# Reordering three pieces of a fused scan and expert kernel: a ScalarE copy in the start, a state update and a gated layer on VectorE

## The chip, the cores and the metric

The kernel runs on one core of a Trainium2 chip. The metric is the device time of one execution in microseconds, as the median of several runs; lower is better. Everything is computed in fp32.

## The reference, cut to what matters

Two stages run one after the other. The first is a gated linear recurrence over time (a "mamba2" scan), computed in chunks. The second is a sum over four expert networks, each weighted by a probability.

```python
# scan: batch 4, 8 heads, 768 steps, head_dim 32, d_state 16
for c in range(nc):                       # per chunk of the sequence
    cum = np.cumsum(log(a)[chunk])
    M = (C @ B.T) * exp(cum_i - cum_j) * causal
    y = M @ x + (C @ state) * exp(cum)
    state = exp(sum) * state + sum_j(B_j x_j * exp(cum_last - cum_j))
...
# experts: 3072 tokens, D = 256, 4 experts, F = 1024
p = probs / (probs.sum(-1) + 1e-9)
for e in range(4):
    h = np.maximum(x @ w1[e], 0.0)
    out += p[:, e:e+1] * (h @ w2[e])
```

The `x` of the second stage is the output `y` of the first, with its heads laid side by side.

## The kernel before, in words

**Tiling.** The 3072 tokens are 24 chunks of 128. Four chunks, one of each sequence, make a block `k` of 512 tokens, so there are six blocks (`NBLK`). A block goes through eight steps (`SPB`): four experts, each in two halves of its hidden layer. A step has the number `n`, 0 to 47, and `r = n % 8` is its place in the block. While the experts of block `k` run, the chunks of block `k + 1` go through the scan in between, so the scan has to be woven into the experts' steps.

**The experts' step.** Each step computes two matrix products by a seven-product (Strassen-like) scheme. The first layer is `fmul(n, 1..7)` (L500, matmuls on L514), which accumulates in two PSUM banks named X and Y. The second layer of the step before is `smul(n - 1, 1..7)` (L584, matmuls on L599), which accumulates in four banks `acc0` to `acc3`. Each of these fourteen products is two 128x256 matmuls with 128x128 weights, and the profile records each matmul as two passes. Between the two layers VectorE and ScalarE do this:

- `snap` (L518): ScalarE copies the bank X as it stands to SBUF.
- `total` (L523, operation on L526): VectorE adds the bank Y and a snap and writes `z`. `total(n, 7, "22")` must have read Y before `fmul(n, 3)` may write on in it.
- `gated` (L528, L536): VectorE takes max(., 0) of its source and multiplies by the gate. `gated(n, "21", "X")` reads the bank X itself; the others, `"12"` among them, read a `z` in SBUF.
- `diff` (L540, L543): VectorE subtracts two gated layers, which gives T1 to T4 for the second layer. T2 and T4 are put in a list `late` and run in the next step, after its first gated layer.

**The scan's parts in the steps.** In steps with r = 0, 2, 4 and 5 a chunk's decays are computed (`decay_part` 0 and 1, scans on L355). In steps with r = 3 and r = 6, called scored here, two chunks are scored: `masks` on ScalarE (L369), `decay_part(c, 2)` on VectorE (two scans `dec`, L338, and on GpSimd `cts`, L341), `scores` on TensorE (L384) and `masked` on VectorE (eight multiplies, L396). `scores` works in four groups of 32 rows, one for each pair of heads, and its four results go into four banks: two of the pool `ps_att`, then Y, then X. So the third group has to wait until `total(n, 6, "12")` has read Y, and the fourth until `gated(n, "21", "X")` has read X. In the steps after (r = 4 and 7) `outputs` (L441, L453) makes the scan's result from them.

**The carried state.** `carry(c)` (L471) makes a chunk's state for the next block: a 32x32 block transpose (L477), from block 1 on a multiply-add with the old state (L479), and a multiply by a mask (L484), all on VectorE. It is put at the end of `late`, one chunk in a step, as long as there are chunks in `states`. In a scored step there is one in n = 3 and n = 6 (chunks 2 and 4), and then in each r = 6 up to n = 30: in n = 3, 6, 14, 22 and 30. The chunks of the last block have no state to hand on, and their `carry` does nothing.

**The start.** Before the steps the first chunks are scanned with little to overlap. `masks(0)`, `scores([0])` and `decays(0)` run first. One of the four score results of a chunk is not multiplied by VectorE: `aside(c, q)` (L398) copies it to SBUF on ScalarE (L403), and GpSimd multiplies it (L404). ScalarE also issues two stores, `acut_d` and `ac_d` (L279), which hold the decays that later chunks load.

**What sets the order.** The program is scheduled by hand (`manual_schedule`): each engine executes its instructions in the order in which these lines issue them, and waits on semaphores where a tile is not yet written or not yet free. SyncE issues the loads, in that same order.

Of the kernel before, what the change touches and what calls it, by code (L numbers as in the profile page):

```python
# [17 lines left out]
def kernel(  # L18
# [295 lines left out]
    def spread(c, homes):  # L314


        s = st[c]
        s["a"] = []
        for q, (pool, tag) in enumerate(homes):
            k = slice(32 * q, 32 * q + 32)  # L320
            b = pool.tile([P, NT * P], FP32, tag=tag, name="a")
            nc.tensor.matmul(  # L322
                out=b, lhsT=ones[k], rhs=a_q[k, c].rearrange("p t s -> p (t s)"),
                start=True, stop=True, tile_position=(32 * q, 0))
            s["a"].append(b)

    def decays(c):
        for part in range(3):
            decay_part(c, part)

    def decay_part(c, part):

        s = st[c]
        if part == 2:
            if c >= CPB:

                s["dec"] = dec = att.tile([HN, P], FP32, tag="dec", name="dec")
                nc.vector.tensor_tensor_scan(  # L338
                    out=dec, data0=s["ah"], data1=zeros, initial=1.0, op0=ALU.mult, op1=ALU.add)
                s["cts"] = cts = att.tile([HN, NT, P], FP32, tag="cts", name="cts")  # L340
                nc.gpsimd.tensor_mul(cts, s["ctm"], dec.unsqueeze(1).to_broadcast([HN, NT, P]))  # L341
            return
        half = NH * P // 2
        if part == 0:
            if c >= SPREAD:
                s["a"] = [s["ab"][:, :half], s["ab"][:, half:]]
            LT = att.tile([P, NH * P], FP32, tag="LT", name="LT")
            s["LT"] = LT.rearrange("p (h s) -> p h s", h=NH)

            s["MT"] = att.tile([P, NH, P + N], FP32, tag="MT", name="MT")  # L350

        LT, w = s["LT"].rearrange("p h s -> p (h s)"), s["a"][0].shape[1]
        n = half // w
        for i in range(n * part, n * part + n):
            nc.vector.tensor_tensor_scan(  # L355
                out=LT[:, i * w:i * w + w], data0=s["a"][i],
                data1=ident.rearrange("p h s -> p (h s)")[:, :w], initial=0.0,
                op0=ALU.mult, op1=ALU.add)
        if part == 1 and c < NCH - CPB:
            nc.gpsimd.tensor_mul(  # L360
                s["MT"][:, :, P:], s["xb"][:, OB:OB + HN].rearrange("p (h n) -> p h n", h=NH),
                s["LT"][:, :, P - 1:P].to_broadcast([P, NH, N]))

    def masks(c):

        s = st[c]
        m = s["ctm"] = att.tile([HN, NT, P], FP32, tag="ctm", name="ctm")
        for t in range(NT):
            nc.scalar.mul(m[:, t], s["xb"][:, OCT:OCT + P], tmask[:, t:t + 1])  # L369

    def scores(cs, homes):

        for c in cs:
            st[c]["g"] = {}
        for r, (pool, tag) in enumerate(homes):
            g = pool.tile([P, len(cs), NT, P], FP32, tag=tag, name="g")
            for j, c in enumerate(cs):
                st[c]["g"][r ^ 2 * turned_round(c)] = g[:, j]
        for j, c in enumerate(cs):
            s = st[c]  # L380
            for r in range(NQ):
                k = slice(32 * r, 32 * r + 32)
                g = s["g"][r ^ 2 * turned_round(c)]
                nc.tensor.matmul(  # L384
                    out=g.rearrange("p t s -> p (t s)"), lhsT=s["xb"][k, OBT:OBT + P],
                    rhs=s["ctm"][k].rearrange("p t s -> p (t s)"),
                    start=(j == 0), stop=True, tile_position=(32 * r, 0),
                    skip_group_check=True)
# [9 lines left out]
    def aside(c, q):  # L398

        s = st[c]  # L400
        h = slice(NT * q, NT * q + NT)
        g = att.tile([P, NT, P], FP32, tag="gs", name="gs")
        nc.scalar.copy(out=g, in_=s["g"][q])  # L403
        nc.gpsimd.tensor_mul(s["MT"][:, h, 0:P], g, s["LT"][:, h])  # L404
# [123 lines left out]
    def gated(n, b, src):  # L528

        if n not in hid:  # L530
            hid[n] = {}
        h = hid[n][b] = ffn.tile([P, JJ, HB], FP32, tag="h" + b, name="h" + b)
        k, e = n // SPB, n % SPB // JJ
        half = int(b[1]) - 1
        g = gate[k, e].rearrange("p c s -> p (c s)")[:, half * HB:half * HB + HB]
        nc.vector.scalar_tensor_tensor(  # L536
            out=h, in0=first[n][src], scalar=0.0, in1=g.unsqueeze(1).to_broadcast([P, JJ, HB]),
            op0=ALU.max, op1=ALU.mult)
# [161 lines left out]
    def leave(k, c):  # L700

        for q in range(P // 32):
            for d in range(2):
                leave_part(k, c, q, d, nc.sync)

    def opened(n):

        fmul(n, 1)
        snap(n, 1)
        fmul(n, 2)  # L710
# [16 lines left out]
    masks(0)  # L727
    scores([0], homes)
    decays(0)
    masks(1)  # L730
    spread(1, banks)
    aside(0, 3)
    masked([0], (2, 0, 1))
    store_decays(0)
    turn_gates(ps_att, "att")
# [65 lines left out]
    late = []  # L801
    states = [2, 3]
    for n in range(PLAIN, NS):
        k, r = divmod(n, SPB)

        ahead = CPB * (k + 1)
        scanned = [ahead + d for d in {0: [0], 2: [1], 4: [2], 5: [3]}.get(r, [])]
        scored = [ahead + d for d in {3: [0, 1], 6: [2, 3]}.get(r, [])]
        done = [ahead + d for d in {4: [0, 1], 7: [2, 3]}.get(r, [])]
        if k == NBLK - 1:  # L810
            scanned, scored, done = [], [], []
        ending = r == 0 and k > 0
        e = r // JJ
        if r % JJ == 0 and n + JJ < NS:
            load_gate(*divmod(n // JJ + 1, E))
        if PLAIN + 2 < n + 2 < NS:
            load_w1(n + 2)
            load_w2(n + 2)
        opened(n)
        total(n, 1, "11")  # L820
        gated(n, "11", "z11")
        for work in late:
            work()
        if r == 1 and k > 0:
            combine(k - 1, 0)
            combine(k - 1, 1)
        for c in scanned:
            decay_part(c, 0)
        for c in scored:
            masks(c)  # L830
        if k > 0 and 2 <= r < CPB + 2:
            leave(k - 1, r - 2)
        smul(n - 1, 1)
        fmul(n, 6)
        snap(n, 6)
        smul(n - 1, 3)
        if ending:
            keep(k - 1, 0)
        if done:
            outputs(done)  # L840
            states.extend(done)
        fmul(n, 5)
        fmul(n, 7)
        snap(n, 7)
        total(n, 7, "22")
        smul(n - 1, 7)
        smul(n - 1, 5)
        if ending:
            keep(k - 1, 1)
        gated(n, "22", "z22")  # L850
        if r == 1 and k > 0:
            combine(k - 1, 2)
        for c in scanned:
            decay_part(c, 1)
        for c in scored:
            decay_part(c, 2)
        if n == PLAIN:
            sum_w2(0, 1)
        elif n == SPB - 4:
            sum_w1(n + 2)  # L860
        elif n >= SPB - 3:
            sum_w2(n)
        if n < CPB:
            load_chunk(n + CPB)
        for c in scanned if n >= CPB else []:
            if c + 2 < NCH:
                load_decays(c + 2)
        for c in done:
            if c + CPB < NCH:
                load_tokens(c + CPB)  # L870
                load_heads(c + CPB)
        fmul(n, 3)
        total(n, 6, "12")
        fmul(n, 4)
        gated(n, "21", "X")
        if not scored:
            gated(n, "12", "z12")
        if r == SPB - 1 and k < NBLK - 1:
            sums(k + 1)
        smul(n - 1, 6)  # L880
        if scored:
            scores(scored, ((ps_att, "att"), (ps_att, "att"), (ps_f, "Y"), (ps_f, "X")))
            masked(scored, (3, 2, 0, 1))
            gated(n, "12", "z12")
        smul(n - 1, 2)
        diff(n, "T3", "22", "12")
        smul(n - 1, 4)
        if n == PLAIN:
            sum_w2(1, 1)
        if n != SPB - 4:  # L890
            sum_w1(n + 2)
        if PLAIN < n < SPB - 4:
            sum_w2(n + 1)
        diff(n, "T1", "12", "11")
        if r == 1 and k > 0:
            turned_out(k - 1)
        late = [lambda n=n: diff(n, "T2", "22", "T1"), lambda n=n: diff(n, "T4", "21", "T2")]
        if states:
            late.append(lambda c=states.pop(0): carry(c))
# [48 lines left out]
```

## Time and profile before

| what | value |
|---|---|
| time, median of 5 runs | 638.64 us (638.58 to 641.01) |
| time of the profiled execution | 639.22 us |
| span of the profiled execution | 637.4 us, so 1.8 us lie around it |
| TensorE busy | 632.5 us, 99% of the span |
| TensorE weight loads busy | 537.2 us, 84% |
| VectorE busy | 483.4 us, 76% |
| ScalarE, GpSimd busy | 119.4 us and 112.0 us, 19% and 18% |
| granted TensorE clock | 1.000 |
| DMA | 190 GB/s over the span |

Times in the profile are microseconds from the start of the span. In the timeline a line gives the start, the time it took, the engine, the line of the kernel, the operation, its output and inputs, their shapes and the number of instructions that were merged. In brackets stands the idle time of the engine before it and what ended that idle time. The recorded end of a matmul is modelled and overlaps the next one, so the distance from start to start tells more of TensorE than the busy time does.

### The profile page before, as it was taken

What the parts mean: (1) busy time and instruction counts of PE and PEld (TensorE: products, weight loads), DVE (VectorE), ACT (ScalarE), POOL (GpSimd) and SP (SyncE); (2) the same over time, 40 slices, a digit from 0 to 9 for tenths busy, and PEclk for the clock granted to TensorE, in tenths of its full rate; (3) what the DMA queues carried; (4) which work ended last, traced back from release to release, by engine and by line L of the source; (5) the groups of instructions that cost most, each with busy time, mean ns of one, the idle gap of its engine ahead of it and who ended that gap; (6) DMA issues with size and microseconds to landing.
All of it is one profiled execution on the core that took longest, in us unless ns stands there. A gap on an engine that the chain in (4) does not pass through costs nothing.

```text
span 637.4 us, 9254 instructions
## 1 busy us (share of the span) xinstructions
PE 632.5 (99%) x3405; PEld 537.2 (84%) x3405; DVE 483.4 (76%) x812; ACT 119.4 (19%) x263; POOL 112.0 (18%) x163
## 2 busy tenths in 40 slices
PE   9999999999999999999999999999999999999997
PEld 5788887888888888888888888888888888888886
DVE  7869988888777788678687778778867677756555
ACT  4011221212111221122221221122111211111110
POOL 5788557020001002100002000000100000100001
PEclk9999999999999999999999999999999999999999
DMA  6998893855666292657284567639365644156001
GB/s 223 277 329 301 280 340 141 294 185 165 182 211 236 79 378 68 236 176 245 100 281 157 170 193 197 233 109 353 88 218 186 221 156 133 62 169 224 1 1 33
DMA packets 98224, 121.61 MB, mean 191 GB/s; under 512 B 29496, under 2 KB 81412, under 8 KB 98180
## 3 DMA queue, kind: packets, MB, share of 16 engines
q1 hardware_dynamic: 95224, 111.20, 53.2%
q0 software_dynamic: 2432, 9.50, 3.9%
q8 instruction: 27, 0.44, 0.3%
q10 hardware_dynamic: 524, 0.32, 0.2%
q14 instruction: 17, 0.14, 0.1%
HBM read 108.16 MB, written 12.83 MB: 190 GB/s over the span
## 4 chain that ended last, share of the span: by engine, by line
PE 98%; DVE 1%; ACT 0%; issue 0%; DVEq 0%
PE acc L599 43%; PE X L514 25%; PE Y L514 19%; PE g L384 2%; PE acc L580 2%; PE y L453 2%; PE X L563 1%; PE Y L563 1%; PE y L441 1%; PE t L720 1%; DVE hT L543 0%; PE a L322 0%; DVE h L536 0%; DVE z L526 0%; PE gp L300 0%
## 5 line engine op out<-in xcount | busy, mean ns | idle before, releaser
L526 DVE TENSOR_TENSOR z<-Y,snap 128x512 f32<-128x512 f32 x138 | 94.6, 685 | 117.2 <-ACT snap L521 66.3
L599 PE MATMUL acc<-hT,wt 128*128 128x256 f32 x736 | 181.0, 379 | 0.0
L521 ACT COPY snap<-X 128x512 f32<-128x512 f32 x138 | 80.8, 586 | 464.6 <-PE X L514 388.1
L599 PEld LDWEIGHTS acc<-hT,wt 128*128 128x128 f32 x736 | 139.8, 190 | 19.0
L599 PE MATMUL acc<-h,wt 128*128 128x256 f32 x552 | 142.5, 381 | 0.0
L514 PE MATMUL X<-yS,wt 128*128 128x256 f32 x552 | 141.7, 379 | 0.0
L599 PEld LDWEIGHTS acc<-h,wt 128*128 128x128 f32 x552 | 104.0, 190 | 17.0 <-issue 2.3
L514 PEld LDWEIGHTS X<-yS,wt 128*128 128x128 f32 x552 | 104.8, 190 | 14.5 <-issue 0.3
L536 DVE SCALAR_TENSOR_TENSOR h<-z,gate 128x512 f32<-128x512 f32 x138 | 99.0, 717 | 3.5 <-PE acc L580 0.4
L514 PE MATMUL Y<-yT,wt 128*128 128x256 f32 x368 | 94.6, 380 | 0.1
L514 PEld LDWEIGHTS Y<-yT,wt 128*128 128x128 f32 x368 | 68.7, 190 | 11.3 <-DVE z L526 0.8
L543 DVE TENSOR_TENSOR hT<-h,hT 128x512 f32<-128x512 f32 x92 | 65.2, 709 | 1.8
L543 DVE TENSOR_TENSOR hT<-h,h 128x512 f32<-128x512 f32 x92 | 65.1, 748 | 1.4
L355 DVE TENSOR_TENSOR_SCAN LT<-ab,ident 128x512 f32<-128x512 f32 x42 | 52.1, 1242 | 0.0
L514 PE MATMUL Y<-yS,wt 128*128 128x256 f32 x184 | 48.3, 385 | 0.0
L514 PE MATMUL X<-yT,wt 128*128 128x256 f32 x184 | 47.2, 379 | 0.0
L360 POOL TENSOR_TENSOR MT<-xb,LT 128x128 f32<-128x128 f32 x20 | 8.5, 427 | 207.4 <-DVE LT L355 102.5
L396 DVE TENSOR_TENSOR MT<-g,LT 128x256 f32<-128x256 f32 x94 | 32.4, 415 | 13.1 <-PE g L384 13.1
L514 PEld LDWEIGHTS Y<-yS,wt 128*128 128x128 f32 x184 | 34.1, 190 | 6.4 <-issue 2.2
L514 PEld LDWEIGHTS X<-yT,wt 128*128 128x128 f32 x184 | 35.0, 190 | 4.8
L536 DVE SCALAR_TENSOR_TENSOR h<-X,gate 128x512 f32<-128x512 f32 x50 | 34.3, 685 | 5.7 <-PE X L514 3.4
L341 POOL TENSOR_TENSOR cts<-ctm,dec 128x256 f32<-128x256 f32 x20 | 14.1, 724 | 129.1 <-DVE dec L338 129.1
(104 smaller groups left out, 324.5 us busy)
## 6 DMA issues: line engine op xcount, KB each, us to landing
wt<-in_w_dram SPq DMA_DIRECT2D x112, 256.0 KB
wt<-w_d SPq DMA_DIRECT2D x40, 640.0 KB
wt<-w_d SPq DMA_DIRECT2D x40, 512.0 KB
ab<-acut_d SPq DMA_DIRECT2D x21, 512.0 KB
gate<-p_d SPq DMA_DIRECT2D x23, 256.0 KB
w_d<-wt POOLq DMA_DIRECT2D x8, 640.0 KB, 4.1
wt<-in_w_dram SPq DMA_DIRECT2D x40, 128.0 KB
xb<-in_xbc_dram SPq DMA_DIRECT2D x14, 320.0 KB
```

The costliest lines, as they stand in the source:

```text
L341: nc.gpsimd.tensor_mul(cts, s["ctm"], dec.unsqueeze(1).to_broadcast([HN, NT, P]))
L355: nc.vector.tensor_tensor_scan(out=LT[:, i * w:i * w + w], data0=s["a"][i], data1=ident.rearrange("p h s -> p (h s)")[:, :w], initial=0.0, ...
L384: nc.tensor.matmul(out=g.rearrange("p t s -> p (t s)"), lhsT=s["xb"][k, OBT:OBT + P], rhs=s["ctm"][k].rearrange("p t s -> p (t s)"), start ...
L396: nc.vector.tensor_mul(s["MT"][:, h, 0:P], s["g"][q], s["LT"][:, h])
L453: nc.tensor.matmul(out=y[32 * q:32 * q + 32, t, 0:w], lhsT=s["xb"][:, h * D:h * D + D], rhs=s["MT"][:, NT * q + t, 0:w], start=(k == 0 and ...
L514: nc.tensor.matmul(out=f[bank][:, j], lhsT=wt1[n][:, w, j * P:j * P + P], rhs=rhs, start=(i in (1, 2, 5) and j == 0), stop=(j == JJ - 1), ...
L521: nc.scalar.copy(out=s, in_=first[n]["X"])
L526: nc.vector.tensor_add(z, first[n]["Y"], first[n][i])
L536: nc.vector.scalar_tensor_tensor(out=h, in0=first[n][src], scalar=0.0, in1=g.unsqueeze(1).to_broadcast([P, JJ, HB]), op0=ALU.max, op1=ALU. ...
L543: nc.vector.tensor_sub(h[o], h[x], h[y])
L563: nc.tensor.matmul(out=f[bank][:, j], lhsT=wt1[n][:, w, j * P:j * P + P], rhs=yT[k][:, i, cols], start=(i == 0 and j == 0), stop=(i == 1), ...
L599: nc.tensor.matmul(out=acc[k, u][:, half], lhsT=w2_op(n, w)[:, j], rhs=rhs[:, j], start=(begins and j == 0), stop=(n % SPB == SPB - 1 and ...
```

## The change

Three pieces of work change their place in the program's order. No instruction is added or removed. TensorE, GpSimd and SyncE keep their order; ScalarE's order changes in the start, and VectorE's in the scored steps.

1. In the start, `aside(0, 3)` moves in front of `masks(1)`. On ScalarE the copy of the fourth score result of chunk 0 then comes before the two masks of chunk 1.
2. In scored steps `carry` no longer runs with T2 and T4, in front of `total(n, 7, "22")`. It runs after that total and the gated layer `"22"`, in front of `decay_part(c, 2)`.
3. In scored steps `gated(n, "12", "z12")` runs before `masked` instead of after it, as it already does in all other steps.

```diff
     decays(0)
+    aside(0, 3)
     masks(1)
     spread(1, banks)
-    aside(0, 3)
     masked([0], (2, 0, 1))
...
         gated(n, "11", "z11")
-        for work in late:
+        for work in late[:2] if scored else late:
             work()
...
         for c in scanned:
             decay_part(c, 1)
+        for work in late[2:] if scored else []:
+            work()
         for c in scored:
             decay_part(c, 2)
...
         gated(n, "21", "X")
-        if not scored:
-            gated(n, "12", "z12")
+        gated(n, "12", "z12")
         if r == SPB - 1 and k < NBLK - 1:
             sums(k + 1)
         smul(n - 1, 6)
         if scored:
             scores(scored, ((ps_att, "att"), (ps_att, "att"), (ps_f, "Y"), (ps_f, "X")))
             masked(scored, (3, 2, 0, 1))
-            gated(n, "12", "z12")
         smul(n - 1, 2)
```

## The prediction

> **What bounds the kernel now.** I read the page first, then TensorE's busy time by stretch, then TensorE's and VectorE's timelines around the changed steps. The page and the stretches:
>
> ```profile
> PE 632.5 (99%) x3405; PEld 537.2 (84%) x3405; DVE 483.4 (76%) x812; ACT 119.4 (19%) x263; POOL 112.0 (18%) x163
> PE 98%; DVE 1%; ACT 0%; issue 0%; DVEq 0%
> ```
>
> ```profile
> 0.00:25.00 25.00, 23.69 (x173) 1.00 0.75 241
> 25.00:110.00 85.00, 84.86 (x472) 1.00 0.81 279
> 110.00:632.40 522.40, 522.40 (x2763) 1.00 0.53 175
> ```
>
> The columns of the second are the stretch, its length, TensorE's busy time, its clock and the DMA share. TensorE is the bound: from 110 us to 632.4 us it has no idle time. There is nothing to gain there, only something to lose. What idleness there is lies in the start (1.31 us) and in block 0's steps (0.14 us recorded).
>
> Of block 0, the chain of waits shows where VectorE gets onto the path, in step 6:
>
> ```profile
> 95.75 1.10 DVE hT L543
> ...
> 97.00 0.49 DVE S L479
> ...
> 97.52 0.29 DVE M L484
> 97.81 0.61 DVE z L526
> ...
> 98.47 1.13 PE Y L514 x4
> ```
>
> T4 (hT), then the carried state (S, M), then `total(6, 7)` (z), and only then does TensorE get the bank Y for `fmul(6, 3)`. TensorE's timeline gives the price. In step 14 the eight passes in front start at 199.90 and Y at 201.63: 1.73 us, or 0.216 a pass. In step 6 they start at 96.44 and Y at 98.47: 2.03, so 0.30 late, and Y's own four passes take 0.97 instead of 0.86. The stall costs 0.41 us. In step 3 it is 1.78 and 0.97: 0.16 us.
>
> Now a later scored step with a carry, number 14, on VectorE and TensorE:
>
> ```profile
> 199.04 0.29 DVE L484 TENSOR_TENSOR M<-S,qmask 128x128 f32<-128x128 f32 x1
> 200.72 0.69 DVE L526 TENSOR_TENSOR z<-Y,snap 128x512 f32<-128x512 f32 x1 [1.38 <-ACT snap L521]
> 201.44 0.69 DVE L536 SCALAR_TENSOR_TENSOR h<-z,gate 128x512 f32<-128x512 f32 x1
> 202.05 0.73 DVE L338 TENSOR_TENSOR_SCAN dec<-ah,zeros 128x128 f32<-128x128 f32 x2
> 202.70 0.68 DVE L526 TENSOR_TENSOR z<-Y,snap 128x512 f32<-128x512 f32 x1
> 203.55 0.69 DVE L536 SCALAR_TENSOR_TENSOR h<-X,gate 128x512 f32<-128x512 f32 x1 [0.17 <-PE X L514]
> 205.52 0.76 DVE L396 TENSOR_TENSOR MT<-g,LT 128x256 f32<-128x256 f32 x2 [1.28 <-PE g L384]
> ```
>
> ```profile
> 204.31 1.15 PE L384 MATMUL g<-ctm,xb 32*128 32x256 f32 x16
> ```
>
> The carry (its last piece is the first line) ends at 199.33, and VectorE then idles 1.38 us until ScalarE's snap lets it do `total(14, 7)`. So before the total the carry is free. After the total there is one idle gap of 0.17 us; then `gated(14, "21")` reads X until 204.24, and 0.07 us later TensorE starts the scores, whose fourth group writes X. There is next to no slack behind the total. The next gap, 1.28 us, comes only after that read.
>
> **What the Trainium skill says.** "TensorE: Matmul & The Clock Gate", The mechanism: matmuls start and end in program order, and only weight loads are pulled ahead. So a fourth group that waits holds up chunk two's scores and all later products. No run here shows that wait yet. "TensorEngine Tiling (Array Packing)", Key Properties: a change of tiling mode drains the array. The trace agrees: the four passes before the scores take 0.96 us to the next start (203.35 to 204.31) and not 0.86; change or not, that is paid. "VectorE: DVE Perf Modes", Two Vector instructions with no wait between them: an instruction that is not held need not wait for the end of the one before. The trace agrees: two independent 0.69 us layers start 0.61 apart (321.88, 322.49). "SBUF — State Buffer", Who interferes with whom: a VectorE instruction with two SBUF inputs contends with a GpSimd instruction that reads SBUF. The trace agrees: T2 and T4 take 2.34 us for two beside GpSimd's weight sums (94.50) and 1.41 alone (197.19).
>
> **The change part by part.**
>
> *The copy in the start.* ScalarE's second masks run from 7.06 (0.69 us); it then idles 0.29 us and copies at 8.04, released by the scores. In front of the masks the copy still starts at 8.04, because the scores are no earlier. Gain 0. The masks now run from about 8.35 to 9.04; the second scores read them at 10.37, so 1.3 us of TensorE's work hides them. Behind the masks on ScalarE's queue stands the store of `acut_d`, issued at 8.11 now and about 8.7 then. SyncE waits 3.7 us for its landing, until 14.20, and issues the decays of chunk 3 and the next weights behind it, so these may come up to 0.6 us later. The decays land at 17.5 and are scanned at 18.95: 1.5 us cover. The copy of `p_sb` (9.29) and the store `ac_d` wait for the transpose and stay. Bounds: +0.3 if a load that I cannot see is short; -0.3 if the tokens of chunk 1, which ended the wait before the masks, land more than the 0.29 us later in other executions. I take 0.
>
> *The carry behind the total.* It removes the stalls of 0.16 and 0.41 us and puts the carry's time in front of the read of X, in five steps. Its price is from start to start: 0.73 us with the multiply-add (328.93 to 329.66 in the timeline, transpose to the next scan), 0.45 without (0.24 transpose to mask, plus 0.21 mask to next).
>
> Step 14 (22 and 30 run alike; 30's rows lie at the same distances): carry at 202.05, scans at 202.78, second total 0.65 later at 203.43, gated 21 0.61 later at 204.04 (X has been complete since 203.5), end 204.73. TensorE starts 0.06 after such an end (step 6: 98.42 to 98.47), at 204.79. The fourth group started at 204.33 before. Loss 0.46 us; three steps, 1.38 us.
>
> Step 6: T4 now leads to the snap's end, 97.23, so the total starts at 97.26, in time for Y. Gated 22 at 97.98, carry 98.59, scans 99.32, total 99.97, gated 21 100.58, end 101.27, fourth group 101.33. Before, stall included, it was 101.28. Net +0.05: the gain of 0.41 is spent again a microsecond later. Step 3: 57.66, 58.38, 58.99, 59.44, 60.09, 60.70, end 61.39, group 61.45 against 61.43. Net +0.02.
>
> Bounds: if the carry costs its full 0.82 us (198.52 to 199.33) and gated 21 follows the total without overlap (0.72 and not 0.61), each of the five steps loses 0.2 more, +1.0. If the released group saves the slower first pass of a drained array (0.32 instead of 0.216), each loses 0.1 less, -0.5. I take the middle.
>
> *The gated layer before the scores' products.* 0.69 us more on VectorE between the read of X and `masked`. It fills the gap of 1.28 us (step 14: 204.65 to 205.34, and `masked` could not start before 205.98). In steps 3 and 6, beside GpSimd, the layer took 1.10 us (65.28); there 0.2 us are left. Without that cover `masked` would be late by what is missing, and the next `fmul` 1, which needs X, still comes 0.94 us after its products end (373.89 against 372.95 in step 11). Cost 0. T3 and T1 come 0.7 us earlier, but TensorE does not wait for them: gain 0.
>
> *Sum.* 1.38 + 0.05 + 0.02 = +1.45 us on the profiled execution: 639.22 to 640.67. It lies 0.58 above the median of the runs, 638.64; the same 1.45 on that gives 640.1. That is +0.23%. About 0.3% (1.9 us) is what a measurement of this kernel can tell from no change.
>
> **The rivals.**
>
> *A, the forecast: the stall moves from Y to X,* 640.1, with its bounds 639.6 to 641.0. Chance 0.47; perhaps a tenth of that lies above 640.56.
>
> *B, slower: the late fourth group also gets out of step.* Place: the scores in the five steps. The four row groups run their passes together (sixteen passes in 1.08 us). If chunk two's passes cannot run beside a late fourth group, one more pass of 0.216 follows in each step: 5 x 0.216 = 1.08, total +2.53, 641.2. It turns the result to slower from 0.1 us a step. For it: matmuls keep their order. Against: in the trace all four groups start within 0.02 us, so they are independent. Chance 0.33.
>
> *C, faster: the read of X is not what the scores wait for,* or carry and scans overlap more. Then the 0.57 us of stalls go and nothing comes back: 638.1. For it: no wait at the fourth group is in the trace. Against: 0.07 us between the read's end and the group in every scored step. Chance 0.13.
>
> *D, the start decides:* the copy or the delayed store moves the first outputs by a microsecond either way, on top of A: 639.1 to 641.1. The recorded waits there speak against it. Chance 0.07.
>
> **How the numbers follow.** A and B hold 0.80: from A's lower bound to B with some of A's bounds, 639.2 to 641.7. Slower by over 0.3%: B (0.33), A's upper tail (0.04) and the upper half of D (0.03), 0.40. Faster by over 0.3%, under 636.7: C with a gain in the start that I do not see, 0.03. The rest 0.57.
>
> **What would show it.** In the profile after: Y at its 1.73 us in steps 3 and 6; in step 14 VectorE's idle gap before the first total grown from 1.38 to about 2.1 us; in steps 14, 22 and 30 TensorE's scores row longer or later by 0.46 us, released by `h` of L536; nothing of the kind in step 11, which has no carry. In the start the copy still at 8.04. The prediction is wrong if the scores in step 14 keep their distance of 0.96 us and length of 1.08.

## The result and the profile after

The changed kernel takes 640.01 us (median of 23 runs, 639.48 to 640.5); the kernel before, run beside it, takes 638.81 us (median of 44 runs). The ratio is 1.0017, with a 95% interval of 1.0012 to 1.0023. That is 1.2 us slower, where 1.45 was forecast: a small loss, clear of the noise, and within the 0.3% that the prediction called no change.

The profiled execution after took 639.97 us (span 638.2) against 639.22 (637.4) before, only 0.75 more. To keep the start, which differs from execution to execution (see the last section), out of the comparison, I measure TensorE's *body* from here on: from the first matmul of L580 in the timeline to the last group of L599 in the chain of waits. Before, that is 632.42 - 23.79 = 608.63 us; after, 633.19 - 23.29 = 609.90. So the body lost 1.27 us and the start of this one execution gained 0.50. The body does not hold the start, so what a change does there is read from the first L580.

The two lines of the page that answer to those of before:

```profile
PE 633.0 (99%) x3405; PEld 537.9 (84%) x3405; DVE 481.9 (76%) x812; ACT 119.2 (19%) x263; POOL 113.4 (18%) x163
PE 98%; DMA 1%; SPq 0%; ACT 0%; issue 0%; POOL 0%; DVE 0%; ACTq 0%; POOLq 0%
```

TensorE's stretches after (length, busy time, clock, DMA share, GB/s):

```profile
0.00:25.00 25.00, 23.26 (x175) 1.00 0.82 259
25.00:110.00 85.00, 85.00 (x475) 1.00 0.80 274
110.00:632.40 522.40, 522.40 (x2747) 1.00 0.54 175
```

VectorE's share of the chain of waits has gone from 1% to 0%, and block 0 has no recorded idle time any more (85.00 of 85.00, before 84.86). By these two views the kernel has improved, and yet it is slower. The loss has to be looked for inside TensorE's "busy" time, in the distance between starts. Step 14 after, VectorE and TensorE:

```profile
200.22 0.69 DVE L526 TENSOR_TENSOR z<-Y,snap 128x512 f32<-128x512 f32 x1 [2.12 <-ACT snap L521]
200.94 0.69 DVE L536 SCALAR_TENSOR_TENSOR h<-z,gate 128x512 f32<-128x512 f32 x1
201.55 0.20 DVE L477 STREAM_TRANSPOSE S<-A 128x32 f32<-128x32 f32 x1
...
202.29 0.73 DVE L338 TENSOR_TENSOR_SCAN dec<-ah,zeros 128x128 f32<-128x128 f32 x2
202.85 1.03 PE L599 MATMUL acc<-hT,wt 128*128 128x256 f32 x4
202.94 0.67 DVE L526 TENSOR_TENSOR z<-Y,snap 128x512 f32<-128x512 f32 x1
203.52 0.68 DVE L536 SCALAR_TENSOR_TENSOR h<-X,gate 128x512 f32<-128x512 f32 x1
203.81 1.57 PE L384 MATMUL g<-ctm,xb 32*128 32x256 f32 x16
...
205.31 1.13 PE L599 MATMUL acc<-h,wt 128*128 128x256 f32 x4
```

and TensorE there before:

```profile
204.31 1.15 PE L384 MATMUL g<-ctm,xb 32*128 32x256 f32 x16
205.39 1.13 PE L599 MATMUL acc<-h,wt 128*128 128x256 f32 x4
```

The idle gap before the first total has grown from 1.38 to 2.12 us, by the carry that left it. The carry (201.55 to 202.29) now stands in front of the read of X (`h<-X`), which ends at 204.20; the 0.17 us of idle time in front of this read is gone. The scores still start 0.96 us after the four passes in front (202.85 to 203.81), but from their start to the next group it is now 1.50 us (203.81 to 205.31) and not 1.08 (204.31 to 205.39): the fourth row group starts late and holds up what follows. The single records of the trace have it: before, its first pass starts 0.02 us after the first group's; after, 0.44 us later (at 204.26, 0.06 us behind the end of the read), and from there to the next group it is 1.06 us in both. TensorE's own view of this line shows no idle time for it, since the other three groups run meanwhile.

This distance, which I call the scores' row, over the ten scored steps:

| step | 3 | 6 | 11 | 14 | 19 | 22 | 27 | 30 | 35 | 38 |
|---|---|---|---|---|---|---|---|---|---|---|
| before, us | 1.08 | 1.08 | 1.08 | 1.08 | 1.08 | 1.08 | 1.08 | 1.08 | 1.08 | 1.08 |
| after, us | 1.22 | 1.50 | 1.08 | 1.50 | 1.08 | 1.50 | 1.08 | 1.50 | 1.08 | 1.08 |

The five longer rows are the five steps that have a carry. Step 6 after:

```profile
95.92 1.89 PE L599 MATMUL acc<-hT,wt 128*128 128x256 f32 x8
96.74 0.69 DVE L526 TENSOR_TENSOR z<-Y,snap 128x512 f32<-128x512 f32 x1 [0.41 <-ACT snap L521]
97.65 1.03 PE L514 MATMUL Y<-yT,wt 128*128 128x256 f32 x4
...
100.04 0.68 DVE L536 SCALAR_TENSOR_TENSOR h<-X,gate 128x512 f32<-128x512 f32 x1
100.33 1.57 PE L384 MATMUL g<-ctm,xb 32*128 32x256 f32 x16
101.83 1.13 PE L599 MATMUL acc<-h,wt 128*128 128x256 f32 x4
```

Y is in time (95.92 to 97.65 is 1.73 us, before 2.03), and the row is 1.50 us. The 0.41 us won at Y is spent again at X, where the row has grown by 0.42.

### The profile page after: what moved, and what is told of

It reads as the page before. It is cut to its first block, busy times and chain, and to the rows that moved or that the text cites. A ratio compares the mean times of both kernels' runs of the same rounds, so it can differ in the third digit from the quotient of the medians.

```text
span 638.2 us, 9255 instructions
## 1 busy us (share of the span) xinstructions
PE 633.0 (99%) x3405; PEld 537.9 (84%) x3405; DVE 481.9 (76%) x812; ACT 119.2 (19%) x263; POOL 113.4 (18%) x163
## 4 chain that ended last, share of the span: by engine, by line
PE 98%; DMA 1%; SPq 0%; ACT 0%; issue 0%; POOL 0%; DVE 0%; ACTq 0%; POOLq 0%
PE acc L599 44%; PE X L514 25%; PE Y L514 19%; PE acc L580 2%; PE g L384 2%; PE y L453 2%; PE X L563 1%; PE Y L563 1%; PE y L441 1%; DMA wt<-in_w_dram 1%; PE gp L300 0%; SPq L120 0%; ACT ctm L369 0%; PE turned L646 0%; SPq L216 0%
## 5 line engine op out<-in xcount | busy, mean ns | idle before, releaser
L599 PE MATMUL acc<-hT,wt 128*128 128x256 f32 x736 | 181.1, 379 | 0.0
L599 PEld LDWEIGHTS acc<-hT,wt 128*128 128x128 f32 x736 | 139.8, 190 | 19.0
L599 PE MATMUL acc<-h,wt 128*128 128x256 f32 x552 | 142.5, 381 | 0.0
L599 PEld LDWEIGHTS acc<-h,wt 128*128 128x128 f32 x552 | 104.0, 190 | 17.0 <-issue 2.0
L536 DVE SCALAR_TENSOR_TENSOR h<-z,gate 128x512 f32<-128x512 f32 x138 | 98.3, 712 | 3.5 <-PE acc L580 0.4
L543 DVE TENSOR_TENSOR hT<-h,hT 128x512 f32<-128x512 f32 x92 | 67.1, 729 | 1.8
L355 DVE TENSOR_TENSOR_SCAN LT<-ab,ident 128x512 f32<-128x512 f32 x42 | 52.1, 1242 | 0.0
L536 DVE SCALAR_TENSOR_TENSOR h<-X,gate 128x512 f32<-128x512 f32 x50 | 34.2, 684 | 4.9 <-PE X L514 2.9
```

Source lines behind the costliest of these rows:

```text
L355: nc.vector.tensor_tensor_scan(out=LT[:, i * w:i * w + w], data0=s["a"][i], data1=ident.rearrange("p h s -> p (h s)")[:, :w], initial=0.0, ...
L536: nc.vector.scalar_tensor_tensor(out=h, in0=first[n][src], scalar=0.0, in1=g.unsqueeze(1).to_broadcast([P, JJ, HB]), op0=ALU.max, op1=ALU. ...
L543: nc.vector.tensor_sub(h[o], h[x], h[y])
L599: nc.tensor.matmul(out=acc[k, u][:, half], lhsT=w2_op(n, w)[:, j], rhs=rhs[:, j], start=(begins and j == 0), stop=(n % SPB == SPB - 1 and ...
```

## The experiments

The theory on trial: VectorE makes two reads that TensorE waits for, the first total (it frees Y) and gated 21 (it frees X). The carry costs its time where it stands in front of one of them without slack. Its main rivals are that the start made the difference, or the gated layer. Bodies are measured as above.

### The three edits one by one

The copy alone:

```diff
     decays(0)
+    aside(0, 3)
     masks(1)
     spread(1, banks)
-    aside(0, 3)
```

> Only the first of the three moves: the copy of the fourth score result of chunk 0 in front of the second masks on ScalarE. My theory: the copy is released by the scores in either order, so the time is that of the kernel before within 0.3 us, and all the scored steps look as they did there (step 6 with its Y 0.30 late, the fourth group never late). Rival (the start gains, as the profile after suggests, whose step 3 begins 0.5 us earlier than that of before): 0.3 to 0.6 us faster.

638.96 us beside 638.87 of the kernel before: ratio 1.0004 (0.9996 to 1.0012). Body 632.37 - 23.74 = 608.63, that of before to the hundredth; all rows are 1.08. ScalarE's timeline of this kernel:

```profile
8.04 0.37 ACT L403 COPY gs<-g 128x256 f32<-128x256 f32 x1 [2.17 <-PE g L384]
...
8.31 0.69 ACT L369 ACTIVATE ctm<-xb,tmask 128x128 f32<-128x128 f32 x2
```

The copy starts at 8.04, as before, since the scores release it: ScalarE now idles 2.17 us in front of it and masks afterwards. The body does not hold this edit, but L580 starts at 23.74, before at 23.79. So the edit is worth nothing that these runs can tell; their interval is -0.3 to +0.8 us.

The carry alone:

```diff
-        for work in late:
+        for work in late[:2] if scored else late:
             work()
...
+        for work in late[2:] if scored else []:
+            work()
         for c in scored:
             decay_part(c, 2)
```

> Only the second move: in scored steps the carried state behind total 7 and gated 22. My theory: this move alone is the loss. Scores rows of 1.50 us in steps 14, 22 and 30 (1.08 before), step 3 and step 6 even, so +1.2 to +1.3 us on the kernel before (ratio about 1.002). Rival (the loss needs the gated layer in front of the products too, since it fills VectorE's gap): rows of 1.08 and 0.57 us faster than before.

639.93 us, ratio 1.0019 (1.0011 to 1.0028); body 633.67 - 23.78 = 609.89, +1.26. Rows 1.21, 1.50, 1.08, 1.50, 1.08, 1.50, 1.08, 1.50, 1.08, 1.08. Its step 14 on TensorE:

```profile
204.30 1.57 PE L384 MATMUL g<-ctm,xb 32*128 32x256 f32 x16
205.79 1.13 PE L599 MATMUL acc<-h,wt 128*128 128x256 f32 x4
```

Here is the whole loss, with the same rows as in the full change.

The gated layer alone:

```diff
         gated(n, "21", "X")
-        if not scored:
-            gated(n, "12", "z12")
+        gated(n, "12", "z12")
...
             masked(scored, (3, 2, 0, 1))
-            gated(n, "12", "z12")
```

> Only the third move: in scored steps gated 12 in front of the eight products. My theory: the layer lies in VectorE's gap of 1.28 us before the products, TensorE never waits for T3 or T1, so the time is that of the kernel before within 0.3 us, with the gap down to about 0.6 us. Rival (the earlier T3 and T1 free VectorE for the next step): up to 0.5 us faster.

638.90 us, ratio 1.0002 (0.9994 to 1.001); body 631.62 - 22.98 = 608.64; all rows 1.08. Step 14 on VectorE:

```profile
203.36 0.68 DVE L536 SCALAR_TENSOR_TENSOR h<-z,gate 128x512 f32<-128x512 f32 x1
204.72 2.41 DVE L396 TENSOR_TENSOR MT<-g,LT 128x256 f32<-128x256 f32 x7 [0.68 <-PE g L384]
```

The layer at 203.36 lies in the gap in front of `masked`, which shrinks from 1.28 to 0.68 us and is still ended by TensorE's scores. TensorE's body stays as it was.

### Take something else away from in front of X

If the queue in front of the read of X is what costs, taking other work out of it must give the loss back. First the two scans `dec` of the scored chunks go behind gated 12 in the changed kernel:

```diff
-        for c in scored:
-            decay_part(c, 2)
...
         gated(n, "12", "z12")
+        for c in scored:
+            decay_part(c, 2)
```

> The changed kernel, with the two scans dec of the scored chunks moved behind gated 12, so that 0.65 us less VectorE work stands in front of the read of X. My theory: any 0.46 us less in front of that read ends the stall, whichever work it is. Scores rows back at 1.08 us in steps 14, 22 and 30, and the stalls of steps 3 and 6 gone as well: 0.5 to 0.6 us faster than the kernel before, 1.7 to 1.9 faster than the changed one. Rival (the fourth group is late because of the carried state itself, by its data or its place): rows stay at 1.50 and the time at +1.2.

639.47 us beside 638.87, ratio 1.0016 (1.0004 to 1.0027; one of the 13 runs took 643.81, and the medians are only 0.60 apart): a miss in the total. In steps 14, 22, 30 and 3 the rows are 1.08, as the theory says. But step 6 went the other way. VectorE, GpSimd and TensorE there:

```profile
97.60 1.63 DVE L536 SCALAR_TENSOR_TENSOR h<-z,gate 128x512 f32<-128x512 f32 x1
97.93 0.74 POOL L180 TENSOR_TENSOR wt<-wt 128x256 f32<-128x256 f32 x1
...
100.46 2.11 PE L384 MATMUL g<-ctm,xb 32*128 32x256 f32 x16
...
102.50 1.13 PE L599 MATMUL acc<-h,wt 128*128 128x256 f32 x4
102.50 1.41 POOL L341 TENSOR_TENSOR cts<-ctm,dec 128x256 f32<-128x256 f32 x2 [0.17 <-DVE dec L338]
```

GpSimd's `cts` waits for `dec`. With `dec` late, `cts` leaves its place in front (it ran at 99.38 in the changed kernel) and the weight sums behind it move up to 97.93, beside gated 22. That layer then takes 1.63 us and not 0.69, the read of X starts at 100.71, 0.67 later than in the changed kernel, and the row is 2.04 (100.46 to 102.50). The page "SBUF — State Buffer" of the Trainium skill, Who interferes with whom, says that a VectorE instruction with two SBUF inputs contends with a GpSimd instruction that reads SBUF. This layer has two, and here it takes more than double its time. The sum against before closes: the Y stalls gone, -0.57; step 6, +0.96; step 4, where the stall at Y is 0.17 because VectorE's work in front of it is slowed beside GpSimd too (a scan of L355 takes 1.74 us and not 1.22); together +0.56. Measured: 632.59 - 23.39 = 609.20, +0.57. The theory holds at X, in step 6 too, where the row is long because the read is late; the miss is a second mechanism that I had not priced: a moved wait on GpSimd sets free what is behind it.

Second, gated 22 goes out of the way, which leaves GpSimd's order and `dec` where they are:

```diff
-        gated(n, "22", "z22")
+        if not scored:
+            gated(n, "22", "z22")
...
         gated(n, "21", "X")
+        if scored:
+            gated(n, "22", "z22")
         gated(n, "12", "z12")
```

> The changed kernel, with gated 22 of the scored steps moved behind gated 21, into VectorE's gap before the products; the scans dec stay in front, so GpSimd keeps its place in time. My theory (what counts is VectorE's work in front of the read of X, and GpSimd must not be set free beside it): 0.61 us less in front, 0.42 needed. Scores rows of 1.08 us in all five steps with a carry, Y on time in steps 3 and 6: 0.5 us faster than the kernel before, 1.7 faster than the changed one. Rival (the products, now behind two layers and the scans' later end, come too late and hold the bank X): a stall at the next step's first product, and no gain on the changed kernel.

638.40 us beside 638.99: ratio 0.9989 (0.9982 to 0.9995), the lowest ratio of all here. All rows 1.08, Y in time in steps 3 and 6; body 631.68 - 23.59 = 608.09, that is 0.54 under before and 1.81 under after (the two stalls are 0.57; the other 0.03 was not followed up). Its step 14:

```profile
200.59 0.20 DVE L477 STREAM_TRANSPOSE S<-A 128x32 f32<-128x32 f32 x1
...
202.82 0.69 DVE L536 SCALAR_TENSOR_TENSOR h<-X,gate 128x512 f32<-128x512 f32 x1 [0.17 <-PE X L514]
...
203.58 1.15 PE L384 MATMUL g<-ctm,xb 32*128 32x256 f32 x16
204.65 1.13 PE L599 MATMUL acc<-h,wt 128*128 128x256 f32 x4
```

The carry stands where the change put it, but the read of X is again released by TensorE after 0.17 us of idle time, and the row is 1.07 to 1.08. So it is not the carry's place behind the total that costs, but that the queue in front of X had no room.

### The cost doubled, in both places

The last multiply of the carry is done twice in scored steps (it writes the same values again), once in the changed kernel and once in the kernel before:

```diff
         nc.vector.tensor_mul(M, S.unsqueeze(1).to_broadcast([HN, NQ, D]), qmask)
+        if again[0]:
+            nc.vector.tensor_mul(M, S.unsqueeze(1).to_broadcast([HN, NQ, D]), qmask)
```

> The changed kernel, with the carry's last multiply done twice in the scored steps (0.21 us from start to start). My theory: work behind the total is paid one for one, so the scores rows of steps 14, 22 and 30 grow from 1.50 to about 1.71 us, those of steps 3 and 6 by the same, and the time by 5 x 0.21 = 1.05 us. Rival (VectorE's order decides, not the amount): rows unchanged, time within 0.3 us of the changed kernel.

In the changed kernel: 642.45 us beside 638.99 (only 4 runs, 641.31 to 643.15), ratio 1.0047 (1.0028 to 1.0066). Step 14:

```profile
204.28 0.29 DVE L486 TENSOR_TENSOR M<-S,qmask 128x128 f32<-128x128 f32 x1
204.61 0.29 DVE L488 TENSOR_TENSOR M<-S,qmask 128x128 f32<-128x128 f32 x1
...
206.01 1.89 PE L384 MATMUL g<-ctm,xb 32*128 32x256 f32 x16
...
207.84 1.13 PE L603 MATMUL acc<-h,wt 128*128 128x256 f32 x4
```

The second multiply adds 0.33 us from start to start, where the expectation had 0.21, the distance from a single multiply to the scans, and the row grows from 1.50 to 1.82; rows 1.54, 1.82, 1.08, 1.82, 1.08, 1.82, 1.08, 1.82, 1.08, 1.08. Body 636.36 - 24.85 = 611.51, +1.61 over after: five times 0.32. What VectorE does in front of X costs one for one. The profiled execution took 643.15, 3.18 more than that of after, and 1.56 of it is a late start (L580 at 24.85, after 23.29), which the last section reads. How much of the median is start can't be said from one profile.

The delay is now long enough for the profile to name the wait, in the view of TensorE's weight loads:

```profile
206.01 0.46 PEld L384 LDWEIGHTS g<-ctm,xb 32*128 32x128 f32 x6 [0.33 <-issue]
206.78 0.72 PEld L384 LDWEIGHTS g<-ctm,xb 32*128 32x128 f32 x10 [0.30 <-DVE h L540]
```

The first six loads are those of the first chunk's other three groups; the fourth group's and all of the second chunk's stand behind the wait for `h`, which is the read of X. Over the kernel this wait is recorded five times, 1.4 us in all, and not once in before or after.

> The kernel before, with the carry's last multiply done twice in the scored steps. My theory: in front of the total the carry is free from step 14 on, since VectorE idles 1.38 us there, so steps 14, 22 and 30 stay as they are; in steps 3 and 6 Y comes later by 0.2 us each (step 6 from 2.03 to about 2.25). Time +0.4 us on the kernel before. Rival (the carry costs the same on either side of the total): +1 us.

In the kernel before: 639.38 us, ratio 1.0007 (0.9999 to 1.0015); body 633.14 - 23.99 = 609.15, +0.52. All rows stay 1.08. Step 14, then step 6:

```profile
200.09 0.29 DVE L488 TENSOR_TENSOR M<-S,qmask 128x128 f32<-128x128 f32 x1
...
201.44 0.69 DVE L530 TENSOR_TENSOR z<-Y,snap 128x512 f32<-128x512 f32 x1 [1.06 <-ACT snap L525]
...
205.03 1.15 PE L384 MATMUL g<-ctm,xb 32*128 32x256 f32 x16
```

```profile
96.84 1.89 PE L603 MATMUL acc<-hT,wt 128*128 128x256 f32 x8
99.19 0.70 PE L518 MATMUL Y<-yT,wt 128*128 128x256 f32 x2 [0.46 <-DVE z L530]
```

In step 14 the second multiply only eats into the idle gap (1.38 to 1.06 us). In step 6 Y comes 2.35 us after the passes in front, where before it was 2.03: +0.32; in step 3 it is +0.20. Their sum is the +0.52 of the body; 0.4 was expected, again with 0.21 for the multiply. The time alone can't tell it from no change. In front of the total the carry is free in three steps and costs in two; behind it, it costs in five.

### The carry behind both reads

Last, the kernel before with the carry behind the read of X, so in front of neither. The scans `dec` of a step now come before its carry, which still reads an older `dec`, so the pool gets four `dec` buffers for two. The copy and gated 12 stand as before.

```diff
-        for work in late:
+        for work in late[:2] if scored else late:
             work()
...
         gated(n, "21", "X")
+        for work in late[2:] if scored else []:
+            work()
```

> The kernel before with the carry of scored steps behind the read of X (behind gated 21, in front of the scores' products) instead of in front of the total, and two more buffers for dec, so that the scans of a step need not wait for the carry of the same step; the copy and gated 12 stand as before. Theory (the two reads of PSUM banks, Y by the first total and X by gated 21, are what TensorE waits for; the carry costs only where it stands in front of one of them on VectorE, and behind both it fills the gap of 1.28 us): Y on its time of 1.73 us in steps 3 and 6, every scores row 1.08 us, TensorE's body 0.57 us shorter than in before, about 638.3, ratio 0.9991. In step 6 GpSimd's weight sums start about a microsecond earlier than in before and may slow the read of X there (0.69 to 1.1 us), which would give back up to 0.4: row of step 6 up to 1.5. Rival (the carry costs its time wherever it stands, or the removal of the stalls is lost to masked): the L599 passes behind the scores or the next fmul 1 late by some tenths in all five steps, 638.8 or more.

638.40 us beside 638.83: ratio 0.9993 (0.9984 to 1.0001), so by the time alone no more than level; but the body, 632.43 - 24.37 = 608.06, is 0.57 under before, exactly the two stalls. All rows are 1.08. Step 14:

```profile
203.57 0.69 DVE L536 SCALAR_TENSOR_TENSOR h<-X,gate 128x512 f32<-128x512 f32 x1 [0.17 <-PE X L514]
204.18 0.20 DVE L477 STREAM_TRANSPOSE S<-A 128x32 f32<-128x32 f32 x1
204.33 1.15 PE L384 MATMUL g<-ctm,xb 32*128 32x256 f32 x16
...
205.54 0.76 DVE L396 TENSOR_TENSOR MT<-g,LT 128x256 f32<-128x256 f32 x2 [0.55 <-PE g L384]
```

The carry fills the gap in front of `masked` (1.28 to 0.55 us), and nothing is late. In step 6 GpSimd's sums slow two of its pieces (the multiply takes 0.86 us there), without effect on TensorE; the read of X, which the expectation feared for, keeps its 0.69. This and the kernel with gated 22 moved are the two ways tried here that keep the 0.57 us, or nearly all of it, that the change wins and gives back.

## Why the prediction was right, step by step

| step of the sum | predicted, us | measured, us | shown by |
|---|---|---|---|
| the copy in the start | 0 | none seen | L580 at 23.74 with the copy alone, 23.79 before |
| Y stalls of steps 3 and 6 | -0.16, -0.41 | -0.16, -0.41 | Y after 1.73 us in both |
| row of steps 14, 22, 30 | +0.46 each | +0.42 each | rows 1.50 for 1.08 |
| row of step 6 | +0.46 | +0.42 | row 1.50 |
| row of step 3 | +0.18 | +0.14 | row 1.22 |
| gated 12 | 0 | 0.00 | the gated layer alone |
| sum | +1.45 | +1.25; body of after +1.27 | |

**The mechanism** is as forecast, rival A's: the stall moves from Y to X. In steps 3 and 6 it is a draw, and the loss is that of steps 14, 22 and 30, where the carry had been free. Of the signs that the prediction named, the release by `h` of L536 is not printed for the changed kernel; with the doubled multiply it is. The copy stood at 7.52 there and not at 8.04, since the scores in front of it were faster in that execution.

**The size** is 0.04 too large in each of five steps. The term that was mis-sized is the distance from the second total to gated 21: I took 0.61 us from two independent layers, and it is 0.58 (202.94 to 203.52), which is 0.03 of the 0.04; the last hundredth is rounding. That the median came so near to the forecast 640.1 is in part luck: the sum was 0.2 too high, and the kernel before measured 638.81 beside it and not 638.64. Two figures of the prediction's range don't follow from its terms: A's upper bound is 641.1 and not 641.0, and the range begins at 639.2 where A's lower bound is 639.6, and the result lies inside either way. The pieces in front came out as written: transpose to scans 0.74 (0.73 predicted), scans to total 0.65 (0.65). "VectorE: DVE Perf Modes" of the Trainium skill, Two Vector instructions with no wait between them, has a held instruction wait until every earlier one has finished; gated 21 starts 0.58 us after a total that takes 0.67, so it was not held. The upper bound, in which it followed without overlap, is thereby out. So is the lower one: from the fourth group's first pass to the next group it is 1.06 us before and after, and no tenth was saved there.

**Rival B** (a further pass of 0.216 us in each row) is out: rows of 1.50 and, with the doubled multiply, of 1.82 are 1.08 plus the delay and nothing more. The page "TensorE: Matmul & The Clock Gate", The mechanism, says that matmuls start in program order. The trace agrees: the group of L599 behind the scores comes later by the same amount, and with the doubled multiply ten loads stand behind the wait, the second chunk's among them. But the second chunk's passes then run beside the fourth group's, and only the delay itself is paid.

**Rival C** (nothing waits at X) is out: rows grow only in the five steps with a carry, they shrink to 1.08 when gated 22 leaves the queue, and with the doubled multiply the profile names the wait. **Rival D** (the start decides) is out as the cause of the loss: the carry alone, with the start as it was, has all of it, and the copy alone has none. The start does vary, though, and the profiled pair shows +0.75 for that reason, not the +1.45 that I set against it.

## What to carry to other kernels

Work that is moved on an in-order engine should be priced at every read behind its new place, for which another engine waits, with the slack of that read; here 0.17 us of idle time in front of the read of X said that 0.7 us more would not fit. A stall that is counted once per early step can come back in all steps of the kind, so each step with the moved piece has to be listed, the quiet ones first. Where a row of matmuls runs in several row groups, neither busy time nor the matmuls' idle time shows that one of them is late: measure from start to start, and look at the weight loads, which showed the wait once the read was late enough.

## What the runs showed of the hardware that was not expected

**The start differs between executions by more than the change is worth.** The first eight score matmuls, from the same start, in the profile of before and in that of the gated layer alone, whose starts are the same program:

```profile
6.66 1.34 PE L384 MATMUL g<-ctm,xb 32*128 32x256 f32 x8
```

```profile
6.66 0.82 PE L384 MATMUL g<-ctm,xb 32*128 32x256 f32 x8
```

The kernel with the copy alone has the slow ones (1.35 from 6.66), the full change and that with the doubled multiply the faster ones (0.82). In the other five they take 0.71, as with the carry alone:

```profile
6.13 0.71 PE L384 MATMUL g<-ctm,xb 32*128 32x256 f32 x8 [0.53 <-ACT ctm L369]
```

The trace keeps a record of the clock that TensorE was granted, and the moment at which it begins, at full speed, goes with this in all ten traces: 10.58 us before and 10.48 with the copy alone; 6.75, 6.76 and 6.17 in the three kernels with 0.82; 4.08 to 4.78 in the five with 0.71. Scores that lie wholly ahead of it take 1.34 or 1.35 us, those more than a microsecond behind it 0.71, and the three between start within 0.3 us of it. No lower clock is recorded there, so that it was lower is inferred from the passes; the 1.00 in the table of stretches counts only what is recorded. Each of the three times occurs with either order on ScalarE, so the change does not choose among them. What sets the moment is open. Nor does it settle the whole start: L580 begins at 23.74 and 23.79 with the slow passes, but anywhere from 22.98 to 24.85 in the other eight.

**A load in the start can hold TensorE up.** In the changed kernel with the doubled multiply:

```profile
20.54 2.34 DVE L355 TENSOR_TENSOR_SCAN LT<-ab,ident 128x512 f32<-128x512 f32 x2 [2.30 <-DMA ab<-acut_d]
...
23.48 1.44 PE L453 MATMUL y<-MT,xb 128*32 128x144 f32 x16 [1.05 <-POOL MT L360]
```

and in the changed kernel itself:

```profile
18.45 2.33 DVE L355 TENSOR_TENSOR_SCAN LT<-ab,ident 128x512 f32<-128x512 f32 x2
...
22.66 0.70 PE L453 MATMUL y<-MT,xb 128*32 128x144 f32 x16
```

The decays of chunk 3 come back from the store `acut_d`; VectorE waits 2.30 us for them, then GpSimd, then TensorE, whose sixteen matmuls take 1.44 us and not 0.70. The doubled multiply first runs in step 3, more than 30 us later, so it is not the cause. The kernel before with the doubled multiply waits 0.86 us at the same place (its L453 takes 1.12). What delays the load is open.

**A waiting instruction can protect another engine.** In the scans' experiment GpSimd's wait for `dec` had kept its sums away from VectorE's layers; without it a layer took 1.63 us and not 0.69.
